# Fetching the first k and q of batch 1 one place earlier in the load queue

## The chip, the cores and the metric

The kernel runs on one core of a Trainium2 chip. Five engines work beside each other, each through its own list of instructions in order: PE (TensorE, matrix products), DVE (VectorE), ACT (ScalarE), POOL (GpSimd) and SP (SyncE, which here only issues loads and stores). Transfers between the chip's memory and the on-chip buffers are carried out by 16 DMA engines. The metric is the device time of one execution in microseconds (us); a change is judged by the median of several runs.

## What is computed

Three layers run one after the other on 4 batches of 576 tokens. The first is attention with 8 heads of size 64 over a window of 64 positions. Its result x enters a layer with 4 experts, each a causal attention of its own, of which every token keeps the two with the largest gates. Its result enters a layer that mixes tokens and channels.

```python
scores = scale * np.matmul(q, k.transpose(0, 1, 3, 2))        # layer 1, window of 64
attn = np.exp(scores) / (np.sum(np.exp(scores), axis=-1, keepdims=True) + 1e-09)
x = np.matmul(attn, v)                                         # 8 heads side by side: 576 x 512
for e in range(4):                                             # layer 2
    q, k, v = x @ wq[e], x @ wk[e], x @ wv[e]
    out += gate[e] * (causal_softmax(scale * (q @ k.T)) @ v @ wo[e])
theta = out @ w_theta                                          # layer 3
y = w_tok_r @ (out * np.cos(theta)) + w_tok_i @ (out * np.sin(theta))
u = out + y
result = u + np.maximum(u @ w_ch, 0.0)
```

## The kernel before

Layer 1 is `phase_a`. It takes the heads in 4 pairs (hp 0 to 3) per batch. For each pair `fetch` loads one tile `qt` (288 KB) and one tile `kt` (320 KB), each from a pool of two buffers; then 3 groups g follow, each with a tile `vt` (192 KB, four buffers). In a group, two copies spread q into a block-diagonal tile `QD` (line 84 on POOL for batches 1 to 3; ACT and DVE do it for batch 0), three products `as` (line 269) make the scores, DVE subtracts the maximum (line 274), ACT takes the exponential (line 282), POOL divides by the sum (line 289, tile `ams`), PE transposes (line 294, `apt`), the result is copied (`apv`), and products with v (lines 147 and 150, `ao`) give a piece of x, which lines 89 and 92 split into a high and a low part (`x0h`, `x0l` for batch 0).

Layer 2 is `qk` and `vg_gates` (products `qk` and `vg` of x with the weights `wih`, `wil`; lines 95 to 97, three products for each because of the split) and `attn` and `wo`. Its weights come through staging tiles `wst` in `load_w`, which are cast on ACT (line 204) and subtracted on POOL or DVE (lines 209 and 211). Layer 3 is `theta`, `mix` and `channel`; its start needs the stored results of layer 2, which line 547 loads back into tiles `ow`.

The pieces of the program are generators that `merge` interleaves by fixed costs: batch 0's `phase_a` runs first with the loading of the first weights; then `qk` and `vg_gates` of batch 0 are interleaved with the first two head pairs of batch 1's `phase_a` and the loading of more weights, and so on. The order in which each engine then executes its instructions is made by a scheduler when the program is built. `tc.issue_after(x)` keeps a load from being placed ahead of x. The list `last_v` holds the v load behind which the q and k of batches 1 to 3 may stand, and `last_load` the latest k load, behind which staging loads may stand.

In names of the trace and of the order below, the number of a buffer is left out or follows an underscore: `kt_638` and `qt_637` are the k and q of batch 1's first pair, `vt_487`, `vt_526` and `vt_561` the three v tiles of batch 0's last pair, `wst_667` the first staging tile of the second set of weights.

Of the kernel before, what the change touches and what calls it, by code (L numbers as in the profile page):

```python
# [25 lines left out]
NP = H // 2  # L26
# [14 lines left out]
def f32(ap):  # L41
    return ap.bitcast(F32)
# [15 lines left out]
def kernel(ctx, tc, qT, kT, vw, consts, w_in, w_o, w_th, w_tk, w_ch, outT):  # L58
# [134 lines left out]
    def load_w(src, n, dst_h, dst_l, tag):  # L193
        for c in range(n):
            h, l = dst_h(c), dst_l(c)
            pool, home = (cp, "zc") if tag == "zc" or tag == "both" and c >= 2 else (bp, "bms")
            st = pool.tile([P, h.shape[1]], F32, tag=home, bufs=2, name=f"wst{c}")
            with tc.issue_after(last_load[0].ins):
                nc.sync.dma_start(st, src[c * P : (c + 1) * P])
            w = h.shape[1]  # L200
            eh, el = KN["WE"][{"zc": 2}.get(tag, 0 if w == W0 else 1)]
            cut = w * eh // 4
            if eh < 4:
                nc.scalar.copy(out=h[:, cut:], in_=st[:, cut:])
            if eh > 0:
                nc.vector.tensor_copy(out=h[:, :cut], in_=st[:, :cut])
            cut = w * el // 4
            if el < 4:
                nc.gpsimd.tensor_sub(out=l[:, cut:], in0=st[:, cut:], in1=f32(h[:, cut:]))
            if el > 0:  # L210
                nc.vector.tensor_sub(out=l[:, :cut], in0=st[:, :cut], in1=f32(h[:, :cut]))
            yield 0.1

    last_load = [None]
    last_v = [None]
    late = [None]
    gated = [None]
    X = {b: xbuf[b % 2] for b in range(B)}
# [3 lines left out]
    def fetch(b, hp):  # L222
        qt = ap.tile([P, D, NB], F32, tag="qt", bufs=2, name=f"qt{b}{hp}")
        kt = ap.tile([P, S + 64], F32, tag="kt", bufs=2, name=f"kt{b}{hp}")
        if b == 0 and hp == 0:

            nc.scalar.dma_start(kt[:, :256], kT[b, hp, :, :256])
            nc.scalar.dma_start(cst[:, : 3 * P], consts[:, : 3 * P])
            nc.sync.dma_start(qt, qT[b, hp])
            last_load[0] = nc.sync.dma_start(kt[:, 256:], kT[b, hp, :, 256:])  # L230
        elif b == 0:
            nc.sync.dma_start(qt, qT[b, hp])
            last_load[0] = nc.sync.dma_start(kt, kT[b, hp])
        else:
            with tc.issue_after(last_v[0].ins):
                last_load[0] = nc.sync.dma_start(kt, kT[b, hp])
                nc.sync.dma_start(qt, qT[b, hp])
        return qt, kt

    def phase_a(b, hps):  # L240
        xh, xl = X[b]
        units = []
        for hp in hps:
            qt, kt = ahead.pop((b, hp)) if (b, hp) in ahead else fetch(b, hp)
            if b == 0 and hp == 0:
                ahead[0, 1] = fetch(0, 1)
            for g in range(3):
                n = f"{b}{hp}{g}"
                vt = ap.tile([P, 3, 2, D], F32, tag="vt", bufs=4, name=f"vt{n}")
                v = nc.sync.dma_start(vt, vw[b, hp, :, 3 * g : 3 * g + 3])  # L250
                if b == 0:
                    last_v[0] = v
                if b == 0 and hp == 0 and g == 2:
                    nc.sync.dma_start(cst[:, 3 * P :], consts[:, 3 * P :])
                if b == 0 and 0 < hp < NP - 1 and g == 0:
                    ahead[0, hp + 1] = fetch(0, hp + 1)
# [432 lines left out]
    for _ in range(WARM):  # L689
        nc.tensor.matmul(warm, mb[:, :P], mb[:, : KN['WM']], start=True, stop=True)  # L690
    merge((20, phase_a(0, (0, 1, 2, 3))),
          (KN["CW"][4], paced((0.75, 0.1, 0.1, 0.1, 0.35), load_w(w_in[:, :W0], NC, lambda c: wih[:, c, :W0], lambda c: wil[:, c, :W0], "both"))))
    pool_mul(mb[:, S - P :], cst[:, 3 * P : 4 * P], 1.0)
    for i in range(2):
        nc.gpsimd.memset(VD[i][0:64, :, 1], 0.0)
        nc.gpsimd.memset(VD[i][64:128, :, 0], 0.0)
    merge((KN["QK"][8], qk(0, 0)), (KN["VG"][0], vg_gates(0)), (KN["PA"][6], phase_a(1, range(KN["AS"][1]))),
          (KN["CW"][5], load_w(w_in[:, W0:], NC, lambda c: wih[:, c, W0:], lambda c: wil[:, c, W0:], "bms")))
    for b in range(B):
        todo = [(KN["AT"][2 * b], attn(b, 0)), (KN["QK"][2 * b], qk(b, 1))]  # L700
        if KN["WOI"] == 2 * b:
            todo.append((KN["CW"][6], load_w(w_o, 2, lambda c: woh[c], lambda c: wol[c], "zc")))
        if b < B - 1:
            todo.append((KN["PA"][2 * b], phase_a(b + 1, range(KN["AS"][b + 1], 4))))
# [113 lines left out]
```

## Time and profile before

| | |
|---|---|
| median of 3 runs | 509.37 us (508.31 to 510.3) |
| the profiled execution | 508.37 us, of which the profile's span is 506.6 us |
| PE busy | 486.7 us, 96% of the span |
| DVE, ACT, POOL busy | 320.9, 323.6, 282.2 us (63%, 64%, 56%) |
| mean granted TensorE clock | 0.996 of full |

The busy time of an engine is the time in which at least one of its instructions was running; PE's is modelled, since products overlap. [...]

### The profile page before, as it was taken

Reading aid. Unit: us, or ns where it says so; the run is one execution under the profiler, and the core shown is the slowest. Engines: PE = TensorE matmul, PEld = TensorE weight load, DVE = VectorE, ACT = ScalarE, POOL = GpSimd, SP = SyncE. Lnnn points to the kernel's source line nnn. Section 1 sums busy time; section 2 is a strip of 40 time slices with the busy share of each in tenths; the row PEclk is TensorE's granted clock in tenths of the full one; section 3 lists DMA queues with packets and bytes.
Section 4 is the critical chain, followed back from the end, with each engine's and each line's share of the span. In section 5 each row is a group of like instructions: output and inputs, shape, how many; then the busy total and the mean of one; then the engine's idle time right before and its main releaser. Section 6 shows DMA issues by size and latency. Waiting matters only on the chain.

```text
span 506.6 us, 11999 instructions
## 1 busy us (share of the span) xinstructions
PE 486.7 (96%) x4188; PEld 455.5 (90%) x4188; DVE 320.9 (63%) x1248; ACT 323.6 (64%) x1031; POOL 282.2 (56%) x446
## 2 busy tenths in 40 slices
PE   7798899999999999999999899999999999999997
PEld 5687888889998999988878699999999999999997
DVE  5766887875977868845897877973453534543312
ACT  7947787876787968858696698863364425523410
POOL 6758799874685872335784457683253514441520
PEclk9999999999999999999999989999999999999999
DMA  7564233431325442111133923321100110011002
GB/s 256 188 205 161 83 123 110 133 113 63 122 84 163 133 142 82 34 47 49 51 112 90 330 87 111 101 76 36 60 2 1 35 60 2 1 47 47 2 1 93
DMA packets 26652, 46.07 MB, mean 91 GB/s; under 512 B 4832, under 2 KB 16096, under 8 KB 26592
## 3 DMA queue, kind: packets, MB, share of 16 engines
q1 hardware_dynamic: 24576, 40.53, 24.9%
q10 hardware_dynamic: 2016, 4.79, 2.8%
q8 instruction: 33, 0.54, 0.5%
q14 instruction: 27, 0.22, 0.1%
HBM read 35.86 MB, written 9.44 MB: 89 GB/s over the span
## 4 chain that ended last, share of the span: by engine, by line
PE 72%; ACT 8%; DVE 7%; DMA 6%; POOL 3%; issue 2%; SPq 0%; POOLq 0%; ACTq 0%; DVEq 0%
PE y L97 8%; PE y L95 8%; PE y L96 8%; PE c L96 3%; PE c L97 3%; PE c L95 3%; PE as L269 3%; DMA w64k<-in_dram 3%; ACT ams L282 3%; PE bpt L470 2%; PE qk L95 2%; PE apt L294 2%; PE qk L96 2%; PE qk L97 2%; DMA wst<-in_dram 2%
## 5 line engine op out<-in xcount | busy, mean ns | idle before, releaser
L92 POOL TENSOR_TENSOR z<-zf,z 128x256 fp32r<-128x256 f32 x72 | 53.4, 759 | 88.0 <-ACT z L89 85.6
L95 PE MATMUL y<-wkh,z 128*128 128x288 f32 x288 | 85.2, 301 | 0.0
L96 PE MATMUL y<-wkl,z 128*128 128x288 f32 x288 | 85.0, 296 | 0.0
L97 PE MATMUL y<-wkh,z 128*128 128x288 f32 x288 | 84.2, 296 | 0.0
L282 ACT ACTIVATE ams<-ams,anm 128x128 f32<-128x128 f32 x144 | 56.6, 397 | 6.2 <-DVE anm L274 4.8
L96 PEld LDWEIGHTS y<-wkl,z 128*128 128x128 f32 x288 | 54.3, 189 | 0.0
L289 POOL TENSOR_TENSOR ams<-ams,arc 128x384 f32<-128x384 f32 x48 | 40.0, 836 | 25.4 <-DVE arc L288 15.5
L97 PEld LDWEIGHTS y<-wkh,z 128*128 128x128 f32 x288 | 53.9, 188 | 0.2 <-POOL z L92 0.2
L95 PEld LDWEIGHTS y<-wkh,z 128*128 128x128 f32 x288 | 53.8, 188 | 0.0
L447 ACT ACTIVATE bms<-bms,bnm 64x64 f32<-64x64 f32 (+4 forms) x80 | 44.7, 560 | 10.7 <-DVE bnm L442 10.2
L84 POOL TENSOR_SCALAR QD<-qt 64x192 f32<-64x192 f32 x72 | 40.1, 557 | 19.7 <-PE as L269 12.8
L581 ACT ACTIVATE ang<-ang 128x256 f32<-128x256 f32 x36 | 14.8, 417 | 50.9 <-DVE ang L580 50.6
L89 ACT CAST z<-zf 128x256 fp32r<-128x256 f32 x72 | 27.4, 403 | 30.7 <-PE y L97 13.3
L596 DVE TENSOR_TENSOR zf<-xk,ang 128x256 f32<-128x256 f32 x64 | 25.3, 419 | 31.9 <-ACT ang L583 20.7
L269 PE MATMUL as<-kt,QD 128*128 128x128 f32 x288 | 41.5, 280 | 4.2 <-ACT x0h L89 1.3
L269 PEld LDWEIGHTS as<-kt,QD 128*128 128x128 f32 x288 | 36.3, 191 | 7.6 <-ACT x0h L89 1.5
L274 DVE CUSTOM_DVE_ANT_0 ams<-as,cst 128x128 f32<-128x128 f32 x144 | 34.9, 283 | 11.0 <-PE apt L294 7.8
L642 DVE SCALAR_TENSOR_TENSOR x2T<-c,x2T 128x288 f32<-128x288 f32 x32 | 14.4, 457 | 36.4 <-PE c L97 36.2
L442 DVE CUSTOM_DVE_ANT_0 bms<-bs,mb 64x64 f32<-64x64 f32 (+4 forms) x80 | 32.5, 422 | 7.6 <-PE bs L440 4.9
L459 POOL TENSOR_SCALAR bpd<-bms,bsm,gw 128x64 f32<-128x64 f32 (+1 forms) x47 | 21.6, 460 | 23.0 <-DVE bsm L452 10.5
L92 POOL TENSOR_TENSOR cu<-x2T,cu 128x288 fp32r<-128x288 f32 x32 | 25.1, 815 | 13.9 <-ACT cu L89 13.8
L438 PE MATMUL bs<-KA,QS 128*128 128x288 f32 (+4 forms) x96 | 31.9, 341 | 0.8 <-DVE bnm L442 0.7
(214 smaller groups left out, 1658.7 us busy)
## 6 DMA issues: line engine op xcount, KB each, us to landing
vt<-in_dram SPq DMA_DIRECT2D x48, 192.0 KB, 3.3
kt<-in_dram SPq DMA_DIRECT2D x15, 320.0 KB, 3.2
qt<-in_dram SPq DMA_DIRECT2D x16, 288.0 KB, 3.4
out_dram<-x2T SPq DMA_DIRECT2D x32, 144.0 KB, 1.8
w64k<-in_dram SPq DMA_DIRECT2D x5, 576.0 KB, 3.8
ow<-od SPq DMA_DIRECT2D x3, 864.0 KB, 5.6
od<-oh SPq DMA_DIRECT2D x8, 288.0 KB, 2.9
od<-ol SPq DMA_DIRECT2D x8, 288.0 KB, 3.6
```

Source lines behind the costliest of these rows:

```text
L84: nc.gpsimd.tensor_scalar(out=out, in0=in_, scalar1=by, scalar2=1.0, op0=ALU.mult, op1=ALU.mult)
L92: eng_l.tensor_sub(out=dst_l, in0=src, in1=f32(dst_h))
L95: nc.tensor.matmul(out, wh, xh, start=first, stop=False)
L96: nc.tensor.matmul(out, wh, xl, start=False, stop=False)
L97: nc.tensor.matmul(out, wl, xh, start=False, stop=last)
L269: nc.tensor.matmul(s[:, i, :], QD[g][:, i], kt[:, 64 * blk : 64 * blk + 128], start=True, stop=True)
L274: nc.vector.tensor_tensor_reduce(out=ms[:, i, :], in0=s[:, i, :], in1=ma0 if (g == 0 and i == 0) else ma1, scale=-0.125, scalar=3.0e38, op ...
L282: nc.scalar.activation(out=ms[:, i, :], in_=ms[:, i, :], func=AF.Exp, bias=nm[:, i : i + 1], scale=-1.0, accum_out=sm[:, i, 0:1],)
L289: nc.gpsimd.tensor_mul(out=ms, in0=ms, in1=rc.unsqueeze(2).to_broadcast([P, 3, P]))
L438: nc.tensor.matmul(s[:m, : z - a], qs[:, q0 : q0 + m], ka[:, a:z], start=True, stop=False)
L442: nc.vector.tensor_tensor_reduce(out=ms[:m, a:z], in0=s[:m, : z - a], in1=mb[:m, mo + a : mo + z], scale=-0.125, scalar=nm[:m, 0:1] if ci ...
L447: ex = nc.scalar.activation(out=ms[:m, :w], in_=ms[:m, :w], func=AF.Exp, bias=nm[:m, ci : ci + 1], scale=-1.0, accum_out=ss[:m, i, 0:1])
```

## The change

Before, `last_v[0]` was overwritten by every v load of batch 0, so q and k of batch 1 stood behind the last one, `vt_561`. Now it has two entries, which only the last head pair of batch 0 sets: groups 0 and 1 set entry 0, group 2 sets entry 1. The fetch of batch 1's first pair uses entry 0, all others entry 1. Since group 1 overwrites what group 0 left, entry 0 is the second v of that pair, `vt_526`. Staging loads in `load_w` now stand behind entry 1 where it is set, in place of the latest k load.

```diff
-            with tc.issue_after(last_load[0].ins):
+            with tc.issue_after((last_v[1] or last_load[0]).ins):
                 nc.sync.dma_start(st, src[c * P : (c + 1) * P])
...
-    last_v = [None]
+    last_v = [None, None]
...
-            with tc.issue_after(last_v[0].ins):
+            with tc.issue_after(last_v[(b, hp) != (1, 0)].ins):
                 last_load[0] = nc.sync.dma_start(kt, kT[b, hp])
                 nc.sync.dma_start(qt, qT[b, hp])
...
-                if b == 0:
-                    last_v[0] = v
+                if b == 0 and hp == NP - 1:
+                    last_v[g == 2] = v
```

The scheduler places later instructions anew as well. On SP, at the end of batch 0's loads, the difference of the two orders is this (a minus is a place before, a plus a place now):

```order
 L250 DMA vt_487<-in_dram 128x384
 L250 DMA vt_526<-in_dram 128x384
-L250 DMA vt_561<-in_dram 128x384
 L236 DMA kt_638<-in_dram 128x640
 L237 DMA qt_637<-in_dram 128x576
+L250 DMA vt_561<-in_dram 128x384
 L199 DMA wst_667<-in_dram 128x256
+L236 DMA kt_851<-in_dram 128x640
+L237 DMA qt_850<-in_dram 128x576
 L250 DMA vt_641<-in_dram 128x384
 L250 DMA vt_741<-in_dram 128x384
```

The k and q of batch 1's first pair moved ahead of one v load, and those of its second pair (`kt_851`, `qt_850`) ahead of the first two v loads of batch 1.

On POOL, where batch 0's last groups end and batch 1's first begin (`ams_534` and `ams_569` are the last two groups of batch 0, `QD_101` to `QD_103` the tiles into which q of batch 1 is spread):

```order
 L289 TENSOR_TENSOR ams_495<-ams_495,arc_503 128x384
+L84 TENSOR_SCALAR QD_101<-qt_637 64x3x64
 L289 TENSOR_TENSOR ams_534<-ams_534,arc_542 128x384
-L289 TENSOR_TENSOR ams_569<-ams_569,arc_577 128x384
-L84 TENSOR_SCALAR QD_101<-qt_637 64x3x64 x2
+L84 TENSOR_SCALAR QD_101<-qt_637 64x3x64
 L84 TENSOR_SCALAR QD_102<-qt_637 64x3x64 x2
 L84 TENSOR_SCALAR QD_103<-qt_637 64x3x64 x2
+L289 TENSOR_TENSOR ams_569<-ams_569,arc_577 128x384
 L209 TENSOR_TENSOR wil<-wst_667,wih 128x64
```

One copy of q now stands ahead of `ams_534`, and five more stand ahead of `ams_569`.

The new places run on through the program up to the start of layer 3; from PE's row 1704 of about 2,920 on, its order is the same again. On PE where layer 3 starts, before (`th` is its first product, `x` and `bpt` belong to batch 3's layer 2):

```order
L96 MATMUL x_5025<-ol_4664,woh_85 128x320
L97 MATMUL x_5025<-oh_4663,wol_87 128x320
L476 MATMUL bdt_4854<-cst,bpd_4824 128x128
L470 MATMUL bpt_4844<-cst,bms_4822 128x128 x3
L470 MATMUL bpt_4850<-cst,bms_4822 128x128
L95 MATMUL th_4984<-wotQS_4762,ow_4966 128x256
```

and now:

```order
L150 MATMUL o_4814<-bpT_4804,vg_3902 64x128 x3
L488 MATMUL o_4814<-bpT_4804,VD_129 128x128
L95 MATMUL th_4984<-wotQS_4762,ow_4966 128x256
L96 MATMUL th_4984<-wotKA_4763,ow_4966 128x256
L97 MATMUL th_4984<-wotQS_4762,ow_4966 128x256
```

The first product of layer 3 stands some 14 products earlier, ahead of nine products `x` and five transposes of layer 2.

## Rows read from the trace of the kernel before

**Rows 1.** The page's first part: span, and PE's busy time.

```profile
span 506.6 us, 11999 instructions
PE 486.7 (96%) x4188; PEld 455.5 (90%) x4188; DVE 320.9 (63%) x1248; ACT 323.6 (64%) x1031; POOL 282.2 (56%) x446
```

**Rows 2.** Stretches: length, then busy PE, PEld, DVE, ACT, POOL; clock, DMA share, GB/s.

```profile
25.00:38.00 13.00, 11.62 (x137) 10.37 (x138) 8.41 (x42) 6.11 (x28) 7.19 (x12) 1.00 0.65 200
38.00:50.00 12.00, 10.18 (x79) 9.45 (x78) 7.89 (x36) 9.16 (x34) 9.76 (x19) 1.00 0.52 169
50.00:63.00 13.00, 12.01 (x113) 11.38 (x110) 10.10 (x51) 9.40 (x37) 9.89 (x19) 1.00 0.28 82
63.00:76.00 13.00, 11.98 (x110) 10.36 (x112) 10.54 (x58) 11.41 (x45) 11.94 (x24) 1.00 0.38 120
76.00:90.00 14.00, 13.45 (x151) 11.32 (x146) 11.11 (x57) 10.76 (x43) 13.48 (x21) 1.00 0.35 102
...
250.00:300.00 50.00, 46.09 (x337) 39.91 (x337) 42.83 (x130) 38.67 (x101) 29.72 (x35) 0.97 0.50 164
```

**Rows 3.** Timeline of SP's queue: start, us, line, instruction.

```profile
24.89 1.48 SPq L250 DMA_DIRECT2D vt<-in_dram  x2
28.86 0.33 SPq L250 DMA_DIRECT2D vt<-in_dram  x1
29.24 1.76 SPq L236 DMA_DIRECT2D kt<-in_dram  x1
31.09 0.38 SPq L237 DMA_DIRECT2D qt<-in_dram  x1
31.52 0.42 SPq L199 DMA_DIRECT2D wst<-in_dram  x1
```

**Rows 4.** Timeline of POOL; in brackets the idle time ahead and what ended it.

```profile
25.84 2.42 POOL L289 TENSOR_TENSOR ams<-ams,arc 128x384 f32<-128x384 f32 x3 [0.82 <-DVE arc L288]
29.71 1.68 POOL L289 TENSOR_TENSOR ams<-ams,arc 128x384 f32<-128x384 f32 x2 [1.45 <-ACT ams L282]
34.54 3.57 POOL L84 TENSOR_SCALAR QD<-qt 64x192 f32<-64x192 f32 x6 [3.15 <-DMA qt<-in_dram]
```

**Rows 5.** Timeline of ACT: the two casts that waited for staged weights.

```profile
34.82 0.40 ACT L204 CAST wih<-wst 128x256 fp32r<-128x256 f32 x1 [3.48 <-DMA wst<-in_dram]
39.16 0.41 ACT L204 CAST wih<-wst 128x256 fp32r<-128x256 f32 x1 [3.22 <-DMA wst<-in_dram]
```

**Rows 6.** Stretches of one microsecond, columns as in rows 2.

```profile
28.00:29.00 1.00, 1.00 (x17) 0.79 (x16) 1.00 (x10) 0.67 (x3) 0.26 (x1) 1.00 0.03 10
33.00:34.00 1.00, 1.00 (x10) 1.00 (x10) 0.00 (x0) 0.00 (x0) 0.00 (x0) 1.00 1.02 368
41.00:42.00 1.00, 0.01 (x1) 0.00 (x0) 0.75 (x3) 0.98 (x4) 0.72 (x1) 1.00 0.45 108
```

**Rows 7.** Timeline of PE: batch 0's last score products, and two waits.

```profile
23.19 0.83 PE L269 MATMUL as<-kt,QD 128*128 128x128 f32 x6
...
35.50 0.39 PE L95 MATMUL vg<-wih,x0h 128*128 128x260 f32 x1 [0.73 <-ACT x0h L89]
...
42.16 0.55 PE L294 MATMUL apt<-cst,ams 128*128 128x128 f32 x3 [1.15 <-POOL ams L289]
```

**Rows 8.** Start of layer 3: `ow` loads and their landing, PE's stretch, first `th`.

```profile
284.08 0.80 SPq L547 DMA_DIRECT2D ow<-od  x2
DMA to landing us min/median/max: 5.6/7.1/8.6
290.00:292.00 2.00, 1.19 (x5) 0.84 1.00 402
292.00:294.00 2.00, 2.00 (x9) 0.50 0.66 271
292.58 1.00 PE L95 MATMUL x<-oh,woh 128*128 128x320 f32 x3
295.35 0.37 PE L95 MATMUL th<-wotQS,ow 128*128 128x256 f32 x1
```

## The prediction, made before the changed kernel was run

> **What bounds the kernel now.** I read the page's first part first. PE is busy for 486.7 of 506.6 us [rows 1], so the whole kernel has 19.9 us in which PE stands still, and a change that adds and removes no work can gain only from those. The view by stretches says where they lie [rows 2]: subtracting PE's busy time from the length gives 1.38 us in 25 to 38, 1.82 in 38 to 50, 0.99 in 50 to 63, 1.02 in 63 to 76, 0.55 in 76 to 90, and 3.91 us in 250 to 300. In between PE hardly stops. The change touches the first of these regions directly and the second only through the new order.
>
> The timelines then say what PE waits for in 25 to 50. SP issues the last v of batch 0 at 28.86, k of batch 1 at 29.24 and q at 31.09 [rows 3]. POOL has finished batch 0 at 29.71 + 1.68 = 31.39 and then stands still for 3.15 us until q lands, 34.5 [rows 4]. ACT waits twice for staged weights, 3.48 and 3.22 us [rows 5]. All of these come through one crowded stretch of transfers: the DMA engines are all but idle at 28 to 29 (share 0.03) and full at 33 to 34 (share 1.02, 368 GB/s) [rows 6]. What PE pays of this directly is 0.73 us at 35.50, for x of batch 0 from ACT, and 1.15 us at 42.16, for the first normalised group of batch 1 from POOL [rows 7].
>
> **The change, part by part.** No arithmetic is added or removed, and the same transfers are made, so the parts are all moves.
>
> The load of k and q. The last v (`vt_561`) is held until 28.86, while the v before it was issued by 24.89 + 1.48 = 26.37 [rows 3]. k and q stood behind that hold. Their own buffers are free sooner: the last score products of batch 0 end at 23.19 + 0.83 = 24.02 [rows 7]. So k can go at about 26.4 in place of 29.24: 2.84 us earlier, at a time when the engines have room. Note that the order shows them behind the second v, not the first; behind the first they could have gone about a microsecond sooner.
>
> When q lands. Issuing k took 1.76 us [rows 3], four times what its neighbours took, and the trace doesn't say why. If that belongs to this place in the queue, q goes at 28.25 and lands at 31.7 (34.54 less 2.84). If it came from the crowd, q goes at 26.8 and, with the same 3.45 us from issue to landing (34.54 - 31.09), lands at 30.25. I keep both ends.
>
> POOL. The first q copy now stands ahead of `ams_534`, and POOL, free at 25.84 + 2.42 = 28.26 [rows 4], waits in front of it until 30.25 or 31.7. A copy takes 3.57 / 6 = 0.60 us and a normalisation 1.68 / 2 = 0.84 us. `ams_534` therefore ends at 31.7 to 33.1, where before it ended at 30.55: 1.1 to 2.6 us late. `ams_569`, with five more copies ahead of it, ends at 31.7 + 5 x 0.60 + 0.84 = 35.5, or at 37.0, where it was 31.39: 4.1 to 5.6 us late. That is the price, and it is paid in x of batch 0. The return is that all six copies are done at 34.7 to 36.1 where it was 38.11, though with one normalisation still to come. Net of that, POOL has the same work done at 35.5 or 37.0 in place of 38.11: 2.6 or 1.1 us ahead. The second q, no longer behind two v loads and the crowd, keeps that lead open.
>
> PE in 30 to 42. Its new order meets `ams_534` after 0.3 us of other products and meets `ams_569` with two groups of batch 1's scores ahead of it, so only part of the lateness is seen. Following the new order with the durations above and q at 30.25: PE waits 0.4 us at the first, about 1 us for the copy behind it, 0.5 us at the second, and starts the products `qk` 1.4 us later than before. It has then done two score groups more (0.9 us of work). The wait of 1.15 us at 42.16 goes, because the first normalised group of batch 1, which ended that wait, is ready at 39.2, 3 us before that wait's end. Adding up, the place that before was reached at 42.5 is reached at 41.15: 1.35 us gained. With q at 31.7 the same steps come out 1.4 us later, which leaves nothing. I take the middle, 0.7 us.
>
> PE in 43 to 90. The idle time left there is about 0.5 (43 to 50) + 0.99 + 1.02 + 0.55 = 3.06 us [rows 2], in stretches in which POOL is the busiest of the helpers (11.94 of 13 and 13.48 of 14 us). A POOL that is 1 to 3 us ahead with batch 1 removes some of these waits, not those for the gates and scores of layer 2, which are not earlier. Bounds: nothing, and all 3.06. I take half, 1.5 us.
>
> The weights. `wst_667` no longer stands behind k and q, only behind `vt_561`: it goes at about 29.3 in place of 31.52, and ACT's first wait ends some 2.2 us sooner. But ACT's new order has this cast ahead of a piece of x (`x0h`) for which it waited for no weights before. What is gained on the one is lost on the other, and it is inside the walk above.
>
> 90 to 245. PE is busy throughout; a lead is carried, nothing is added to it.
>
> 245 to 306, the start of layer 3. The first `th` needs `ow`, whose two loads were issued from 284.08 on in 0.80 us; the slower one takes 8.6 us to land [rows 8], so it is there at about 293.1 (issued in the middle of the row), and PE came to `th` at 295.35, 2.2 us later. In the new order about 2.8 us of products have gone from ahead of it (292.58 to 295.35 at the lower clock, [rows 8]). PE would come to it at about 292.6 and wait 0.5 us. Bounds: if the 0.81 us in which PE stands still at 290 to 292 goes as well, 0.8 us; if they grow, none. I take 0.4 us lost. Other moves in this region I can't price; they are as likely to add as to remove, and the 3.91 us of idle time there [rows 2] bounds what they can remove.
>
> **Sum.** 0.7 + 1.5 - 0.4 = 1.8 us gained. The profiled execution took 508.37 us, 1.0 us less than the median of 509.37, and 1.8 off it makes 506.6; against the median that is 507.6 us, 0.35% less. A measurement of this kernel tells about 0.5% from no change, 2.5 us; so the likeliest case lies inside that.
>
> [...] In all the 250 to 300 stretch lost 3% of 50 us of clock, 1.5 us. [...]
>
> **Rivals.**
> *More than I count.* All 1.35 us, all 3.06 us and the 1.5 us of clock near 292, because the start of layer 3 falls otherwise: 5.9 us, 503.5 us. For it: POOL is the busiest helper up to 90. Against it: it needs three good ends at once.
> *Nothing arrives.* q lands at 31.7, and the waits up to 90 were for layer 2: 0 to 0.5 us, 509. For it: PE's named waits in 25 to 90 come to less than 5 us and only 1.15 of them is POOL's. This is also what is seen if the fetch, being only one place earlier, does too little.
> *Slower.* POOL's new order holds back batch 0. `ams_569` is late by 5.6 us, and on ACT the last piece of x stands behind three staged weights, the last of them 256 KB; the `qk` products of the second half, which need it, stand 3 us behind the wait at 35.50 now and would come 3.5 us later or more. If PE has nothing to fill that with, it loses 3.0 to 3.5 us and the lead on POOL returns only 0.5: 512.1 us. It decides from the point where PE stands still in 30 to 43 for more than 5.5 us (before: 1.38 + about 1.3). Against it: the new order has put two more score groups and several `vg` products in that place.
> [...]
>
> **Chances.** Forecast (0.5 to 3.5 us gained) 0.45; more than that 0.17; nothing, with the clock's case, 0.16; slower by 2.5 us or more 0.22. The border of 0.5% (506.8) lies inside the first case, 0.8 us from its middle; I give 0.22 of its 0.45 to faster. So faster 0.39, same 0.23 + 0.16 = 0.39, slower 0.22. The range reaches from the best end, 503.5 less half a microsecond for the unpriced moves, to the slower case: 503.0 to 512.0. The forecast's own range is 505.9 to 508.9.
>
> **What would show it.** k issued at about 26.4; q landing between 30 and 32; POOL's idle time in front of the first q copy near 2 to 3.4 us, and `ams_569` ending at 35 to 37; PE idle in 25 to 43 no more than now, in 43 to 90 about 1.5 us less than 3.06; the same PE row that stands at 90 now reached 2 us sooner; at `th` a wait of under a microsecond for `ow`. I am wrong if PE stands still longer in 30 to 43 than before, if the lead at 90 is not there, or if the lead is there and lost again after 245.

## The result, and the profile after

The changed kernel took 512.94 us (median of 7 runs, 511.93 to 513.49), the kernel before 509.11 us beside it. The ratio is 1.0072, with a 95% interval of 1.0053 to 1.0091: 0.7% slower, where 0.35% less time was forecast. The profiled execution took 513.02 us.

The page's first part of the changed kernel, beside [rows 1]:

```profile
span 511.2 us, 12009 instructions
PE 490.7 (96%) x4188; PEld 456.9 (89%) x4188; DVE 324.2 (63%) x1248; ACT 323.8 (63%) x1031; POOL 281.4 (55%) x446
```

The span is 4.6 us longer. PE stands still for 20.5 us in place of 19.9, and is busy for 4.0 us more with the same products. So most of the loss is not idle time. The stretches of the changed kernel (columns as in [rows 2]):

```profile
25.00:38.00 13.00, 10.83 (x126) 8.73 (x125) 8.16 (x48) 8.02 (x39) 9.02 (x15) 1.00 0.78 235
38.00:50.00 12.00, 12.00 (x106) 11.38 (x106) 10.16 (x48) 10.60 (x40) 11.21 (x20) 1.00 0.50 146
50.00:63.00 13.00, 13.00 (x139) 12.71 (x140) 10.14 (x54) 9.17 (x37) 10.56 (x22) 1.00 0.26 76
63.00:76.00 13.00, 12.08 (x106) 10.10 (x105) 10.26 (x45) 10.15 (x35) 11.41 (x23) 1.00 0.46 140
76.00:90.00 14.00, 13.40 (x156) 11.91 (x154) 12.02 (x69) 11.59 (x48) 12.78 (x22) 1.00 0.39 113
90.00:250.00 160.00, 158.12 (x1524) 145.08 (x1524) 116.04 (x526) 120.89 (x421) 91.69 (x159) 1.00 0.28 89
250.00:284.00 34.00, 31.31 (x222) 26.48 (x222) 27.81 (x89) 23.76 (x69) 20.89 (x28) 1.00 0.41 119
284.00:306.00 22.00, 19.01 (x120) 15.69 (x120) 18.01 (x46) 16.64 (x38) 9.15 (x8) 0.84 0.53 191
```

The stretches of before that were not shown yet:

```profile
90.00:250.00 160.00, 159.13 (x1544) 146.35 (x1543) 116.39 (x542) 123.37 (x428) 94.43 (x165) 1.00 0.29 92
250.00:284.00 34.00, 31.67 (x238) 27.69 (x239) 27.95 (x93) 25.53 (x74) 20.79 (x27) 1.00 0.45 137
284.00:306.00 22.00, 20.42 (x154) 17.72 (x152) 17.58 (x45) 18.78 (x44) 13.31 (x11) 0.92 0.47 174
```

Subtract busy PE from the length in each, and compare with [rows 2]. From 25 to 90 us the changed kernel stands still for 2.17 + 0 + 0 + 0.92 + 0.60 = 3.69 us, where before it was 5.76: 2.07 us gained. From 90 to 250 it is 1.88 against 0.87, from 250 to 284 2.69 against 2.33, from 284 to 306 2.99 against 1.58: 2.78 us lost. In the last of these the mean clock is 0.84 of full in place of 0.92, which is 0.08 x 22 = 1.8 us more lost to half clock. All seven executions of the changed kernel had a mean granted clock of 0.990 to 0.996, the 23 of the kernel before that were timed beside run 10 below 0.993 to 1.000. What is left of PE's 4.0 us, some 2.2, lies inside its busy time where the clock reads 1.00. Some 0.6 of it stands ahead of 8 us, where the two orders are still the same: the first 18 score products took 2.89 us in this execution and 2.25 in that of before. That is a difference of the two executions and not of the change. Of PE's groups the score products `as` grew most, from 41.5 to 44.1 us for the same 288 products, these 18 among them; why the others grew was not settled.

At the head, SP, POOL and PE of the changed kernel read like this (timelines as in [rows 3], [rows 4] and [rows 7]):

```profile
26.98 0.43 SPq L236 DMA_DIRECT2D kt<-in_dram  x1
27.50 0.37 SPq L237 DMA_DIRECT2D qt<-in_dram  x1
29.43 0.33 SPq L250 DMA_DIRECT2D vt<-in_dram  x1
29.80 0.42 SPq L199 DMA_DIRECT2D wst<-in_dram  x1
30.28 0.42 SPq L236 DMA_DIRECT2D kt<-in_dram  x1
30.81 1.80 SPq L237 DMA_DIRECT2D qt<-in_dram  x1
...
31.45 0.54 POOL L84 TENSOR_SCALAR QD<-qt 64x192 f32<-64x192 f32 x1 [2.62 <-DMA qt<-in_dram]
31.96 0.82 POOL L289 TENSOR_TENSOR ams<-ams,arc 128x384 f32<-128x384 f32 x1
32.87 2.94 POOL L84 TENSOR_SCALAR QD<-qt 64x192 f32<-64x192 f32 x5
35.89 0.83 POOL L289 TENSOR_TENSOR ams<-ams,arc 128x384 f32<-128x384 f32 x1
...
32.84 0.55 PE L294 MATMUL apt<-cst,ams 128*128 128x128 f32 x3 [0.77 <-POOL ams L289]
```

k is issued at 26.98 in place of 29.24 and q is there at 31.45 in place of 34.54. POOL waits 2.62 us for it. `ams_534` ends at 32.78 and `ams_569` at 36.72; PE pays 0.77 us for the first of them.

At the start of layer 3 the changed kernel's PE, DVE and ACT, to be held against [rows 8] (`bnm` is the maximum that layer 2's softmax subtracts, `bms` its tile, `wtuk` and `w64k` belong to the conversion of a mixing weight):

```profile
291.73 0.41 PE L95 MATMUL x<-oh,woh 128*128 128x320 f32 x1 [1.07 <-DVE bnm L442]
...
293.26 0.66 PE L470 MATMUL bpt<-cst,bms 128*128 128x128 f32 x2 [0.83 <-DVE bms L459]
...
295.35 0.56 PE L95 MATMUL th<-wotQS,ow 128*128 128x256 f32 x1
...
289.33 1.84 DVE L127 SCALAR_TENSOR_TENSOR wtuk<-w64k,wtuk 128x576 uint32<-128x576 uint32 x1
291.10 0.15 DVE L452 RECIPROCAL bsm<-bsm 128x2 f32<-128x2 f32 x1
...
279.43 0.59 ACT L89 CAST wotQS<-wot 128x512 fp32r<-128x512 f32 x1 [1.90 <-PE wot L97]
...
284.22 0.74 ACT L119 ACTIVATE wtuk<-w64k 128x576 f32<-128x576 f32 x1 [2.56 <-DMA w64k<-in_dram]
```

The first `th` starts at 295.35, to the hundredth as before, and waits for nothing. But the nine products `x` and five transposes that stood ahead of it are still to be done. PE stood still in 290 to 293 for two waits on layer 2's last softmax, and the half clock now lasts longer: by single microseconds the clock reads 0.50 from 293 to 299, where before it was 0.50 from 292 to 294. The `th` products behind the first take 0.41 us in it, and 0.28 or 0.29 before, at 1.00. The second of the two waits has its like in the kernel before:

```profile
291.18 0.57 PE L470 MATMUL bpt<-cst,bms 128*128 128x128 f32 x2 [0.81 <-DVE bms L459]
```

What is new is the first, 1.07 us for a `bnm` where before it was 0.46 at 288.84, and some short waits ahead of it. ACT waits 1.90 us for the products `wot`, and 2.56 us (0.45 before) for a mixing weight whose load it issues behind that, at 280.26 in place of 278.58.

### The profile page after: what moved, and what is told of

Read it like the earlier page. It is cut to its first block, busy times and chain, and to the rows that moved or that the text cites. A ratio compares the mean times of both kernels' runs of the same rounds, so it can differ in the third digit from the quotient of the medians.

```text
span 511.2 us, 12009 instructions
## 1 busy us (share of the span) xinstructions
PE 490.7 (96%) x4188; PEld 456.9 (89%) x4188; DVE 324.2 (63%) x1248; ACT 323.8 (63%) x1031; POOL 281.4 (55%) x446
## 4 chain that ended last, share of the span: by engine, by line
PE 75%; ACT 9%; DVE 9%; DMA 3%; issue 2%; POOL 2%; SPq 0%; DVEq 0%; POOLq 0%; ACTq 0%
PE y L95 7%; PE y L97 7%; PE y L96 7%; PE as L269 5%; PE c L96 3%; PE c L97 3%; PE c L95 3%; PE qk L95 3%; PE qk L96 2%; PE qk L97 2%; PE ao L150 2%; PE bs L438 2%; DVE bms L442 2%; PE apt L294 2%; ACT ams L282 2%
## 5 line engine op out<-in xcount | busy, mean ns | idle before, releaser
L269 PE MATMUL as<-kt,QD 128*128 128x128 f32 x288 | 44.1, 287 | 3.4 <-ACT x0h L89 1.3
L459 POOL TENSOR_SCALAR bpd<-bms,bsm,gw 128x64 f32<-128x64 f32 (+1 forms) x47 | 20.4, 436 | 23.5 <-DVE bsm L452 7.7
L438 PE MATMUL bs<-KA,QS 128*128 128x288 f32 (+4 forms) x96 | 30.8, 333 | 0.6 <-POOL KA L84 0.3
```

Of the source, the lines that this page charges most:

```text
L269: nc.tensor.matmul(s[:, i, :], QD[g][:, i], kt[:, 64 * blk : 64 * blk + 128], start=True, stop=True)
L438: nc.tensor.matmul(s[:m, : z - a], qs[:, q0 : q0 + m], ka[:, a:z], start=True, stop=False)
```

## The experiments

**How orders were written out.** The scheduler places the whole program anew when one load is held differently. To separate the load from the new places, most kernels below have the order of every engine written out: a function run at the program's end puts each instruction behind the one that is to stand ahead of it on its engine. This fixes issue order alone and adds no wait on a result.

```diff
-    kp.release()
+    pin(nc, tc); kp.release()
...
+def pin(nc, tc):
+    import base64, zlib
+    by = {i.name: i for i in nc.cur_bb.bb.instructions}
+    for row in zlib.decompress(base64.b85decode(ORDER)).decode().split("|"):
+        row = [by[k] for k in ("I-" + n for n in row.split(",")) if k in by]
+        for prev, i in zip(row, row[1:]):
+            tc.add_manual_dep(i, prev.name, mybir.DependencyInfo(
+                mybir.DependencyClass.NoSync, mybir.DependencyReason.DATA), reason="pin")
```

With the table of the kernel before, the changed source gives the order of before on every engine, instruction for instruction; with its own, its own. No run times one of the two kernels with nothing but its own order written out. Run 7 comes near: it is the changed kernel's order with seven instructions moved, and its time is that of the changed kernel. A kernel "with the seam at 250" has, engine by engine, everything that had started by 250 us in one kernel's trace in that kernel's order, and then the rest in the other's.

**1. Half of the change: k and q alone.**

```diff
-            with tc.issue_after((last_v[1] or last_load[0]).ins):
+            with tc.issue_after(last_load[0].ins):
                 nc.sync.dma_start(st, src[c * P : (c + 1) * P])
```

> Only the k and q of batch 1's first pair go behind the second v; the staged weights stand behind the latest k load as before. Theory A (the cost lies where layer 3 starts, in the order that the scheduler happens to write there, and the early k and q are a gain by themselves): the lead of about 2 us at 63 to 140 us is there again; the end then depends on the order at 284 to 306 alone, so anything from 0.995 to 1.008 of before, and the loss against the lead is found in that stretch. Theory B (batch 0's last groups are late, and that is what costs): slower by the same 0.7%, with no lead at 90. Theory C (the edit of the staged weights costs): 0.996, faster.

Measured: 512.66 us, ratio 1.0070 (1.0045 to 1.0096). Slower like the whole change. In this kernel PE's clock fell at the head, to a mean of 0.80 in 30 to 38 us. This stretch, and below it that of the changed kernel (the clock is the third number from the end):

```profile
30.00:38.00 8.00, 6.45 (x63) 5.44 (x63) 4.28 (x19) 3.19 (x14) 4.88 (x9) 0.80 0.81 254
```

```profile
30.00:38.00 8.00, 6.63 (x72) 5.25 (x71) 3.67 (x22) 3.48 (x16) 6.01 (x11) 1.00 0.85 254
```

So the lead that theory A expected was not to be had in it: 0.20 x 8 = 1.6 us of clock went there. Theory C falls. Taken by itself the run is what theory B expected, the same loss with no lead; runs 2 to 4 speak against that. Nor are k and q all that moved: since the staged weights still stand behind the latest k load, the first of them went ahead of the last v too.

**2. The other half: the staged weights alone.**

```diff
-            with tc.issue_after(last_v[(b, hp) != (1, 0)].ins):
+            with tc.issue_after(last_v[1].ins):
```

> Only the staged weights stand behind the last v in place of the latest k load; k and q are fetched as before. SP's order up to 50 us differs from before in one staged weight that goes four places earlier, so the head can hardly differ. Theory A: PE reaches the same work at 90 us within half a microsecond of before; the whole time differs from before, if at all, by what the new order does after 200 us, 0.995 to 1.008. Theory B: 1.000, since batch 0 isn't held back. Theory C: 1.007.

Measured: 513.88 us, 1.0101 (1.0080 to 1.0123), the slowest of all, though no k, q or v moved at the head and one staged weight moved by four places. PE lost time at 43 to 50, at a mean clock of 0.76, and elsewhere:

```profile
43.00:50.00 7.00, 4.50 (x22) 4.13 (x23) 4.80 (x22) 5.05 (x19) 5.04 (x10) 0.76 0.07 11
```

The time lies above what each of the three theories allowed. The lower clock is not what makes this kernel slow: the profiled execution is the slowest of the six (517.48 us, at a mean clock of 0.986), and two others took 513.19 and 512.59 us at 1.000 and 0.999. By its sign this would speak for theory C, but run 1 without this edit is slow as well. What the two have in common is that everything behind was placed anew. That the head would hardly differ was wrong.

**3 and 4. The two orders, put together at 250 us.** Beside that function and its table no line of the program differs from the changed kernel.

> The changed kernel, with each engine's order written out: the order of the changed kernel for all that had started by 250 us, then the order of the kernel before. Theory A: the start of layer 3 takes what it took before, the time is 0.65 us less than before or equal to it, 0.997 to 1.001. Theory B and any theory by which the early fetch itself costs: 1.006 to 1.008, as the changed kernel.

Measured: 508.79 us, 1.0012 (0.9995 to 1.0028).

> The mirror: the order of the kernel before for all that had started by 250 us, k and q of batch 1 fetched behind the last v again, then the order of the changed kernel. Theory A: slower by the 3.5 to 4 us that the start of layer 3 lost, 1.006 to 1.009. Theory B and any theory by which the early fetch itself costs: 0.998 to 1.002.

Measured: 512.50 us, 1.0075 (1.0050 to 1.0100). Both are what theory A said of them: with k and q early and the old order from 250 us on, nothing is lost; with k and q late and the new order from 250 us on, all of the 0.7% is. But in run 3 nothing is gained either: the lead of the head is gone.

**5. The same seam at 140 us.**

> As the run with the seam at 250 us, but with the seam at 140: the order of the changed kernel for all that had started by 140 us, where its lead on PE was about 2.5 us, then the order of the kernel before. If the lead was lost by the changed kernel's order between 140 and 250 us, it now stays and arrives at the start of layer 3: 0.994 to 0.997 of before. If it is lost because layer 2's last softmax steps set the pace there whatever PE has in hand, the lead is there at 240 and gone at 260, and the time is 0.998 to 1.002.

Measured: 510.83 us, 1.0048 (1.0028 to 1.0067), outside of both cases. The trace shows why: at the seam PE waits for a group that the other order had placed elsewhere,

```profile
144.41 0.52 PE L294 MATMUL apt<-cst,ams 128*128 128x128 f32 x3 [3.52 <-DVE x0l L92]
```

so this run says nothing of where the lead goes. It does say what a seam can cost.

**6. The fetch alone.** The order of before on all engines, and on SP one thing moved. SP's order, against before:

```order
 L250 DMA vt_526<-in_dram 128x384
-L250 DMA vt_561<-in_dram 128x384
 L236 DMA kt_638<-in_dram 128x640
 L237 DMA qt_637<-in_dram 128x576
+L250 DMA vt_561<-in_dram 128x384
 L199 DMA wst_667<-in_dram 128x256
```

> The kernel before with the order of every engine written out as it was, and one thing moved: on SP, k and q of batch 1's first pair stand ahead of the last v of batch 0. Nothing is moved on PE, ACT, DVE and POOL. POOL is free at 31.4 us and q lands at 31.5, so its wait of 3.15 us for q falls to some tenths. If the forecast's term for the early q is right, PE's wait of 1.15 us at 42 goes and some of the idle time up to 90 us: 0.995 to 0.999. If an early q is worth nothing by itself: 1.000. If pushing the last v back costs what q gains: 1.002 or more.

Measured: 506.72 us, 0.9966 (0.9950 to 0.9982): faster, by 0.0034 x 508.20 = 1.7 us. POOL and PE of this run:

```profile
30.19 1.68 POOL L289 TENSOR_TENSOR ams<-ams,arc 128x384 f32<-128x384 f32 x2 [1.45 <-ACT ams L282]
31.84 3.78 POOL L84 TENSOR_SCALAR QD<-qt 64x192 f32<-64x192 f32 x6
...
40.99 0.55 PE L294 MATMUL apt<-cst,ams 128*128 128x128 f32 x3 [0.31 <-POOL ams L289]
...
294.19 0.37 PE L95 MATMUL th<-wotQS,ow 128*128 128x256 f32 x1
```

POOL's wait of 3.15 us for q is gone, batch 0's last two groups are not held back, PE's wait of 1.15 us at 42.16 is 0.31, and its wait of 0.73 at 35.50 is not there. (The second pair's q is now waited for: 1.74 us on POOL at 37.77, where before it was 0.42 at 38.94.) PE in 25 to 43 and in 43 to 90:

```profile
25.00:43.00 18.00, 16.71 (x184) 14.92 (x181) 12.47 (x59) 11.70 (x48) 12.53 (x20) 1.00 0.68 211
43.00:90.00 47.00, 44.00 (x416) 39.17 (x414) 37.08 (x193) 37.05 (x146) 41.17 (x76) 1.00 0.35 105
```

It stands still for 1.29 and 3.00 us, before for 2.71 and 3.05. The lead of 1.2 us (40.99 for 42.16) is still 1.2 us at the first `th` (294.19 for 295.35); this execution's head ran 0.48 us late, which makes it 1.7.

**7. One softmax ahead of a weight's conversion.** The changed kernel's order; on ACT (and alike on DVE and POOL):

```order
 L89 CAST wotQS_4800<-wot_4766 128x512
+L447 ACTIVATE bms_4822,BS_117<-bms_4822,bnm_4831 128x448
 L119 ACTIVATE wtuk_4937<-w64k_4936 128x576
 L120 ACTIVATE wtuk_4937<-w64k_4936 128x576
-L447 ACTIVATE bms_4822,BS_117<-bms_4822,bnm_4831 128x448
```

> The changed kernel with its own order written out, except for seven instructions of one softmax of layer 2's last block (batch 3, bms of 448 keys) that stand ahead of the conversion of a mixing weight on three engines: the exponential on ACT, the sum, the reciprocal and two scalings on DVE, two scalings on POOL. No PE instruction and no load is moved. If this conversion in front of the softmax is what made PE wait at 291.7 and 293.3 us, the transposes start at about 291 in place of 293.26, and with them comes a shorter half-clock stretch: 2 to 3.5 us less than the changed kernel, 1.000 to 1.003 of before. If the start of layer 3 is late for another reason (theta put ahead of the nine products, the load of ow): within 0.5 us of the changed kernel, 1.006 to 1.008.

Measured: 512.07 us, 1.0071 (1.0047 to 1.0094): as slow as the changed kernel. The scaling on DVE came 3.5 us earlier (289.11 for 292.64), but PE waited for another thing, for as long as in the changed kernel, since the DVE step that frees the buffer of its next scores now stood behind a step of the conversion:

```profile
291.85 0.47 PE L438 MATMUL bs<-KA,QS 128*128 128x288 f32 x1 [1.34 <-DVE bnm L442]
...
289.50 1.66 DVE L121 TENSOR_SCALAR wtuk<-wtuk 128x576 uint32<-128x576 uint32 x1
...
289.45 1.40 POOL L135 TENSOR_TENSOR wkl<-wtuk,wkh 128x576 fp32r<-128x576 f32 x1 [0.93 <-ACT wkh L134]
```

That step took 1.66 us, beside a POOL instruction, where the like step at 288.13 of the changed kernel took 0.45 (the last section comes back to this).

**8. The seam at 66 us,** a place where the two orders have come close to each other.

> The order of the changed kernel for all that had started by 66 us, on every engine, then the order of the kernel before. By 63 us the changed kernel had about 2.5 to 3 us in hand on PE against before, the fetch alone 1.7. If the new order of the head is worth the difference and an order that is left alone carries it: 0.993 to 0.995 of before. If only the early q is worth anything: 0.9966, as the fetch alone. If the seam makes PE wait for what the two orders place differently, some us more, to be seen as a wait at 66 to 80 us.

Measured: 506.32 us, 0.9956 (0.9939 to 0.9973). The lowest time of all, 2.2 us less than before; the interval does not part it from run 6. A score product of layer 2 and the first `th`:

```profile
242.24 0.27 PE L438 MATMUL bs<-KA,QS 128*64 128x64 f32 x1
...
291.34 0.37 PE L95 MATMUL th<-wotQS,ow 128*128 128x256 f32 x1
```

The same score product in the kernel before, and in the changed kernel:

```profile
244.96 0.27 PE L438 MATMUL bs<-KA,QS 128*64 128x64 f32 x1
...
245.40 0.44 PE L438 MATMUL bs<-KA,QS 128*64 128x64 f32 x2
```

That is 2.7 us of lead at 242 in run 8, and none in the changed kernel, which comes 0.44 us late. `th` comes 4.0 us earlier in run 8, more than the lead; in this execution the clock is 1.00 all through 284 to 306, where before its mean was 0.92.

**9. k and q ahead of the second v too.**

```order
 L250 DMA vt_487<-in_dram 128x384
+L236 DMA kt_638<-in_dram 128x640
+L237 DMA qt_637<-in_dram 128x576
 L250 DMA vt_526<-in_dram 128x384
 L250 DMA vt_561<-in_dram 128x384
-L236 DMA kt_638<-in_dram 128x640
-L237 DMA qt_637<-in_dram 128x576
```

> As the fetch alone (orders written out, nothing else moved), but k and q stand one place earlier still, ahead of the second v of batch 0's last pair. If q's landing is all that counts, POOL is no longer waiting for it when it comes free at 31.4 us and nothing more is gained: 0.996 to 0.998. If the crowd of transfers counts, a little more: 0.995. If the second v, now half a microsecond to a microsecond later, holds up batch 0's last products: 0.998 to 1.002.

Measured: 507.55 us, 0.9979 (0.9967 to 0.9991). Still faster than before, not more than run 6: q is no longer what POOL waits for, and PE pays a wait of 0.92 us at 51.70 (for ACT's `apv`) that run 6 doesn't have. In the profiled execution a lower clock followed as well: its mean is 0.87 in 63 to 76 us, 0.13 x 13 = 1.7 us.

**10 and 14. Placed anew with no load moved.**

(one entry of the table's line)

```diff
-'QK': [16.78, 11.97, 9.28, 7.37, 6.82, 0.65, 9.6, 19.46, 20.6]
+'QK': [16.78, 11.97, 9.6, 7.37, 6.82, 0.65, 9.6, 19.46, 20.6]
```

> The kernel before with one number of its table of costs changed, batch 1's part of QK from 9.28 to 9.6, and no load moved: SP's order is the same throughout, all engines stand as before up to some 140 us, and are placed anew from there to layer 3. If being placed anew is what costs, whatever the cause (the table of costs fits the one order that it was chosen with), slower by 0.3 to 1%. If the loss of the changed kernel belongs to the early fetch, 0.998 to 1.002.

Measured: 509.41 us, 1.0023 (1.0007 to 1.0039).

```diff
-'VG': [6.74, 4.28, 3.79, 19.87]
+'VG': [6.74, 4.28, 3.9, 19.87]
```

> The kernel before with another number of its table of costs changed, batch 2's part of VG from 3.79 to 3.9; no load on SP moves, all engines stand as before up to some 190 us and are placed anew from there on. If any new placing costs because the table was chosen with the old one: 1.002 to 1.010. If new placing is as likely to gain as to lose: 0.995 to 1.005 with no preference, and the changed kernel's loss is bad luck of one order.

Measured: 509.31 us, 1.0019 (1.0004 to 1.0034). Run 10 lies between its two answers, run 14 inside the second of its own and just below the first. Both are a little slower, and lose at the same place, the start of layer 3, where PE's idle time is 3.10 and 3.32 us in place of 1.58:

```profile
284.00:306.00 22.00, 18.90 (x139) 15.97 (x138) 17.34 (x33) 17.72 (x40) 10.55 (x8) 0.92 0.52 195
...
284.00:306.00 22.00, 18.68 (x138) 15.83 (x137) 17.46 (x33) 17.73 (x40) 10.53 (x8) 0.92 0.50 188
```

(the first row is of run 10, the second of run 14).

**11 and 12. The seam at 284 and at 270 us.**

> As the run with the seam at 250 us, with the seam at 284. The changed kernel lost some 3.6 us between 284 and 306. If the order of that stretch alone costs it: 0.999 to 1.003 of before. If what stands between 250 and 284 (the mixing weights that are loaded and converted later) costs it: 1.005 to 1.008.

Measured: 512.14 us, 1.0071 (1.0052 to 1.0090).

> As the runs with the seam at 250 (1.001) and at 284 us (1.007), with the seam at 270. If the order that costs stands between 270 and 284, where the changed kernel has a score product of layer 2's last block behind a group of twelve products wot: 0.999 to 1.003. If it stands between 250 and 270: 1.005 to 1.008.

Measured: 510.04 us, 1.0038 (1.0024 to 1.0053). Neither answer of the second expectation: leaving out run 5, with the seam at 66, 250, 270, 284 us and no seam the ratio is 0.9956, 1.0012, 1.0038, 1.0071 and 1.0072. The trace of run 12 speaks for its first answer all the same. Its row at the seam, and the stretch of layer 3's start in run 12 and below it in run 11:

```profile
270.55 0.33 PE L476 MATMUL bdt<-cst,bpd 128*128 128x128 f32 x1 [0.75 <-DVE ol L92]
...
284.00:306.00 22.00, 19.71 (x151) 16.58 (x150) 18.67 (x49) 18.57 (x41) 12.14 (x9) 1.00 0.55 204
...
284.00:306.00 22.00, 18.70 (x129) 16.28 (x129) 18.00 (x45) 16.92 (x38) 10.31 (x9) 0.84 0.55 202
```

The wait of 0.75 us is the seam's own, as in run 5; neither the kernel before nor the changed kernel has it. From 284 to 306 PE stands still for 2.29 us in run 12 and for 3.30 in run 11, and the mean clock of a whole execution is 0.997 to 1.000 in the twelve of run 12 and 0.992 or 0.993 in the six of run 11. So what costs at 284 to 306 seems to be decided ahead of 284, and most of it between 270 and 284. Run 11 alone doesn't show it: its two longest waits there, 1.39 us at 290.11 and 1.11 at 293.03, are not those of the changed kernel, and part of them may be its seam's.

**13. The scores ahead of `wot`.** On PE, in the changed kernel's order (ten instructions on three engines in all):

```order
 L527 MATMUL woT_4705<-cst,wo_4703 128x128 x4
+L438 MATMUL bs_4786<-KA_4284,QS_4283 128x320
+L440 MATMUL bs_4786<-KL_133,QS_4283 128x320
 L95 MATMUL wot_4714<-wth,woT_4691 128x512
```

> The changed kernel with its own order written out and ten instructions moved: on PE the two score products bs of 320 keys (279.23 us) go ahead of the twelve products wot that start at 276.39; on ACT two exponentials and the two loads of mixing weights (280.26 and 280.81) go ahead of the cast of wot, on DVE one sum, reciprocal and two scalings ahead of the subtraction for wot. No load on SP moves. If the late scores are what makes these loads and with them the start of layer 3 late: loads issued near 278.5, 1.5 to 3.5 us less than the changed kernel, 1.000 to 1.004 of before. If not, or if another wait takes its place as with the softmax that was put first: 1.006 to 1.008.

Measured: 511.61 us, 1.0059 (1.0040 to 1.0078), against 1.0072 of the changed kernel: the intervals overlap, so a gain is not shown. The two loads went out at 279.27 and 279.82, 1 us earlier and not 1.7, and PE's two waits are the same as in the changed kernel:

```profile
291.72 0.41 PE L95 MATMUL x<-oh,woh 128*128 128x320 f32 x1 [0.95 <-DVE bnm L442]
...
293.25 0.41 PE L470 MATMUL bpt<-cst,bms 128*128 128x128 f32 x2 [0.82 <-DVE bms L459]
```

## Why the prediction was wrong

**The terms at the head held.** k was issued at 26.98 (forecast 26.4; the whole head of this execution ran 0.56 us late, its `ams` row at 26.40 for 25.84). Issuing it took 0.43 us and not 1.76, so the prediction's second case held: q went right behind k, at 27.50. From issue to landing q took 3.95 us in place of 3.45. A long issue stands in the queue still, now that of the second pair's q, 1.80 us at 30.81; why is not settled. q landed at 31.45 (30.25 to 31.7), POOL waited 2.62 us (2 to 3.4), `ams_534` and `ams_569` ended at 32.78 and 36.72 (31.7 to 33.1, and 35.5 or 37.0), and the six copies at 35.81 (34.7 to 36.1). PE stood still for 2.17 us in 25 to 43, where before it was 2.71, and for 1.52 in 43 to 90, where before it was 3.05. That is 0.54 and 1.53 us gained, where the sum has 0.7 and 1.5. The walk to the first of them was not as told: of its waits PE paid 0.77 for `ams_534` (forecast 0.4), 0.30 for a piece of x, and none for the copy behind it (about 1) or for `ams_569` (0.5). That the sum came so near is in part luck.

Run 6 shows that the fetch by itself is worth this, 1.7 us, and by another road: without the copies ahead of `ams_534` and `ams_569`, both waits of [rows 7] shrink, 1.42 us less idle time in 25 to 43, and nothing more is gained up to 90. The forecast's 0.7 there was too low and its 1.5 was not the early q's but the new order's.

**The step that failed is the one called "90 to 245"**: that a lead is carried and nothing is added to it. It is carried when the order behind it stays as it was: 1.2 us from 42 to 295 us in run 6, and 2.7 us at 242 in run 8. In the changed kernel's own order PE stood still 1.01 us more from 90 to 250 and 0.36 more from 250 to 284, and the score product that run 8 has 2.7 us early at 242 is 0.44 us late: the lead of the head was gone before layer 3, not lost after 245 as the prediction's sign of being wrong has it. Between run 8 and run 3, which differ in the order from 66 to 250 us, lie 0.0056, 2.8 us, of which 2.3 us are idle time in 63 to 250; which places in between carry it stays open. Runs 8, 3 and 11 together make the sum that the prediction should have had: 2.2 us gained up to 66, 2.8 lost from there to 250, 3.0 lost to what stands between 250 and 284, 3.6 lost in all, where 3.7 were measured; what the seams themselves cost is in it. The prediction saw in the order that the places change up to layer 3, and priced only two spots of it.

**The second step is the start of layer 3**, the term of 0.4 us. It was sized by one wait, that of `th` for `ow`. That wait didn't come. What came was 1.41 us more idle time and 1.8 us more lost to half clock in 284 to 306: 3.2 us. Runs 3 and 4 show that the order from 250 us on decides this. Run 11 has the old order of `th` and `x` back and loses as much, and run 12 puts most of the loss down to what stands between 270 and 284. By these runs theory A, which put the cost into the order at the start of layer 3, had the place of the loss and not that of its cause. Attempts to find one group of instructions that carries it failed (runs 7 and 13): a wait that was taken away came back as another. It stays open which places ahead of 284 carry it.

**"As likely to add as to remove" was wrong for the moves that were not priced.** Five programs were placed anew by the scheduler, three with a held load and two with one number of the table of costs changed, and all five were slower than before: 1.0072, 1.0070, 1.0101, 1.0023, 1.0019. In 284 to 306 us PE stands still for 2.41 to 3.32 us in these five, and for 1.58 in before. But they are not five independent draws. Read by line, operation and tile, the traces of runs 1, 2, 10 and 14 have one and the same order on PE, ACT, DVE and POOL from some 245 us on, so at the start of layer 3 there are two new orders here, and both lose. An order that is better than its neighbours can only get worse by being shuffled; that the table of costs was chosen with it is the likely reason, and is argued, not shown.

**The rivals.** The one called slower named 512.1 us, near what came, by a mechanism that did not happen: PE stood still for 1.37 us in 30 to 43, and not for more than 5.5 (before it is 2.06 there; the prediction's 1.38 + about 1.3 is that of 25 to 43). Its 512.1 also lies just outside the prediction's own range, which ends at 512.0. The chances count with "nothing" a case of the clock, a lower one at the head of the changed kernel. No run shows what lowers it. In the changed kernel the clock is 1.00 all through 25 to 90, though PE stands still for 1.37 us in 30 to 38. In run 1 it was 0.80 in 30 to 38, with 1.55 us of idle time, in run 2 it was 0.76 in 43 to 50, with 2.50, and at 292 to 300 of the changed kernel its mean is 0.57, with 0.83. But run 4's profiled execution has 0.82 us of idle time in the same 292 to 300, at a clock of 1.00. At the start of layer 3, where the forecast left a longer half clock out, it was worth 1.8 us.

## What to carry to other kernels

An edit to a kernel whose instructions a scheduler places is two edits: the one that was meant, and a new order for all that follows. Measure them apart: write the old order out, move only the thing meant, and keep that if it gains (here 0.34% faster, where the same fetch left to the scheduler is 0.70% slower in run 1, and the whole edit 0.72%). Where the old order was chosen among many, be ready for a loss from a new one, above all at a place that lives on small waits, such as the start of a stage; and don't call the unpriced moves even.

## What was not expected of the hardware

The same program, with the same order on every engine, was granted the full clock in some executions and less in others: the six of run 4 went from 510.44 us, at a mean granted clock of 1.000, to 514.08 us, at 0.989. So part of a median is how many of its executions had the lower clock.

One instruction on DVE took 2.5 times as long as its equals. In the changed kernel the five steps `wtuk` of line 127 from 262 us on were

```profile
L127 DVE SCALAR_TENSOR_TENSOR wtuk<-w64k,wtuk x5: 749/750/1839, 261.9 to 304.2; 128x576 uint32<-128x576 uint32 x5
```

(least, median and most, in ns). The slow one, at 289.33, ran beside a POOL instruction of line 135 that started at 289.15 and took 1.41 us. It stood ahead of the reciprocal for which layer 2's last softmax waited. It ended at 291.17, 0.61 us after POOL's instruction did. In the kernel before, a step of line 127 that started at 257.00, beside line 135's at 256.60 (1.63 us), took 1.85 us and ended 0.62 us after it. In 230 to 306 us of the two traces nine DVE steps of the lines 121, 127 and 459 took over 1 us. Each of them started 0.01 to 0.40 us after a POOL instruction of line 129 or 135 had started, and ended 0.05 to 0.62 us after that one's end. Beside POOL's scaling of line 459, which ran from 261.78 for 1.33 us in the changed kernel, it was otherwise: the step of line 127 at 261.94, all of it beside that scaling, took 0.75 us. Why the nine were slow is not shown.

Such a slow step is not peculiar to the changed kernel. In the kernel before it is the softmax's own scaling, beside a POOL instruction of 1.40 us that started at 289.51:

```profile
289.53 1.60 DVE L459 TENSOR_SCALAR bms<-bms,bsm,gw 128x384 f32<-128x384 f32 x1
```

The same scaling took 0.48 us in the changed kernel (at 292.64), and PE's 0.81 us at 291.18 are a wait for the slow one. In run 7, which took the step of line 127 out of the softmax's way, the step of line 121 was slow in its place, and the `bnm` for which PE waited stood behind it. So it is not shown that these slow steps cost PE its waits, nor is it excluded: no run here was made to take them away.
